# When the background work of a retention and two-FFN kernel is issued, and on which engine: a reckoned clock for each engine, GpSimd kept to the head

## The chip, the cores and the metric

The kernel runs on one core of one Trainium2 chip. The metric is the device time of one execution in microseconds (us); lower is better. The five engines run side by side: TensorE (PE) multiplies matrices, VectorE (DVE), ScalarE (ACT) and GpSimd (POOL) work on elements, and SyncE (SP) starts most DMA transfers. Each engine takes its own instructions strictly in the order in which the program issued them, so that an instruction that waits holds up everything behind it on its engine.

## The reference

```python
def _attn_ref(q, k, v):                     # 2 x 8 heads x 768 x 64
    gamma = 1.0 - 2.0 ** (-5.0 - np.arange(H, dtype=np.float32))
    for t in range(S):
        state = gamma * state + einsum('bhd,bhe->bhde', k[:, :, t], v[:, :, t])
        y[:, :, t] = scale * einsum('bhd,bhde->bhe', q[:, :, t], state)

def _moe_ref(x, w_a, w_b, w_out):           # 1536 tokens, 512 -> 1536 -> 512
    return (x @ w_a) * (x @ w_b) @ w_out

def _moe2_ref(x, w_gate, w_val, w_out, rms_g):
    xn = x / sqrt(mean(x * x, axis=-1) + 1e-06) * rms_g
    return silu(xn @ w_gate) * (xn @ w_val) @ w_out
```

Retention feeds the first feed-forward layer (FFN1, a product of two projections), whose output is normalised and goes through the second (FFN2, with a SiLU gate). The weights arrive as 64-bit integers that hold the bits of the numbers.

## The kernel before

**Precision.** A product of two float32 matrices is made of three matmuls: each operand is split into a high part, rounded to TensorE's fp32r format (`xh`, `uh`, `oh`, `hh`), and a low part, the rest (`xl`, `ul`, `ol`, `hl`). The high part is an ACT copy, the low part a subtraction on VectorE or GpSimd.

**The head** is the retention: twelve chunks of 128 tokens, with scores (`sc`, masked into `p`), a state (`st`) and results (`ya`), mixed with the first two blocks of FFN1. It ends near 77 us.

**The two FFNs** have 12 blocks `f` of 128 hidden columns each, taken in pairs. For the token blocks `j` = 0 and 1 (512 tokens each) a block is a *slot*: seven products P1, P2, P6, P7, P5, P3, P4 of sums and differences of operands, which stand for the eight of the plain method. P1, P6, P5 and P3 share one PSUM bank (A0 or A1), P2 has B0, P7 and P4 have B1. In the rows these banks are called `b`. Between P6 and P5, and between P5 and P3, ACT and VectorE must take the bank's contents (`t`) before TensorE writes on. For `j` = 2 a block is a *unit* of four plain products, a1 and a2 into one bank and b1 and b2 into a second (both `c` in the rows); the second bank of the unit is B0 before. VectorE multiplies the two into `g`. Twelve *down* products `D` of the pair before go into three banks Y0 to Y2 (`y`), which VectorE adds to the sums `acc` (ACT and VectorE copy in turn where a sum begins). Each product is six matmuls of 128x512. An even slot has the downs between its products, an odd slot has none.

**Background work** is written as generators: `conv_up` and `conv_plain` make float32 values out of the integers (`to_float`: two ACT conversions into `wt` or `u` and `v`, then three VectorE operations), form the sums of weights that the slots need (`wt`, blocks of 256 columns) and split them. `prep_t` forms and splits the differences of the tokens (`xf` or `acc` into `th`, `tl`, `xl`). `tick()`, called after every product, takes steps from the list of tasks, in order of their due times, as long as no engine's sum of estimated costs is further than LEAD beyond TensorE's. `until` forces tasks where a product needs what they make. `norm` is the normalisation between the FFNs; it runs beside the last block of FFN1, with sums of squares in `sq`.

The first set of four downs to open an FFN2 sum is a copy into an `acc` tile that held FFN1's output; `collect` therefore waits with `until` for whoever still reads that tile.

Of the kernel before, what the change touches and what calls it, by code (L numbers as in the profile page):

```python
# [16 lines left out]
P = 128  # L17
# [18 lines left out]
IDLE, LEAD = 1000, {"vec": 300, "act": 300, "gps": 3000}  # L36
# [18 lines left out]
OUTS = 3  # L55
URGENT = NF + 0.5
RS = 5
SECOND = (0, 1), (1, 1), (0, 0), (0, 2), (1, 0), (1, 2)
WAIT = 3, 2
# [4 lines left out]
def retention_glu_swiglu(ctx: ExitStack, tc: tile.TileContext, qk, kv, dq, mask, dg, eye, w1, w2, rg, out):  # L64
    nc = tc.nc

    work = dict.fromkeys(("pe", "vec", "act", "gps"), 0.0)

    class Engine:
# [15 lines left out]
    vec, act, gps = Engine(nc.vector, "vec", 150, 1.0), Engine(nc.scalar, "act", 200, 0.75), Engine(nc.gpsimd, "gps", 50, 2.3)  # L85

    def mm(out, *a, **k):
        work["pe"] += 13 + 0.4 * out.shape[-1]
        nc.tensor.matmul(out, *a, **k)  # L89
# [30 lines left out]
    for f0 in range(0, 2 * NF, G):  # L120
        ups_of = [f0 + 1] + [f0 + 2] * (f0 > 0)
        kinds += [(f, s) for f in ups_of if f < 2 * NF for s in range(2)] + [(f, 2) for f in range(f0, f0 + G)] + [(f0 + 2, s) for s in range(2) if f0 == 0]
# [16 lines left out]
    def to_float(f, s, u, follow=True):  # L139
        while (f, s) not in raws or lock:  # L140
            yield "wait"
        lock.append(f)
        raw = raws.pop((f, s)).rearrange("p (k n) t -> p k n t", k=2)
        lower, upper = raw[:, :, :, 0], raw[:, :, :, 1]
        v = cp.tile([P, DM], I32, tag="r", bufs=RS, name=f"v{f}_{s}").rearrange("p (k n) -> p k n", k=2)
        ui = u.bitcast(I32)
        act.activation(u, upper.bitcast(F32), AF.Copy, scale=2.0 ** -112)
        act.activation(v, lower.bitcast(U32), AF.Copy, scale=2.0 ** -29)
        yield
        vec.tensor_scalar(ui, ui, 3, 0x7FFFFFFF, op0=ALU.logical_shift_left, op1=ALU.bitwise_and)  # L150
        vec.scalar_tensor_tensor(ui, upper, SIGN, ui, op0=ALU.bitwise_and, op1=ALU.bitwise_or)
        if follow:
            load_w()
        yield
        add(ui, ui, v)
        lock.clear()

    def conv_plain(f, s, follow=True):
# [3 lines left out]
        u = cp.tile([P, DM], F32, tag="r", bufs=RS, name=f"u{f}_{s}").rearrange("p (k n) -> p k n", k=2)  # L162
        yield from to_float(f, s, u, follow)
        yield
# [10 lines left out]
        yield  # L175
# [6 lines left out]
    def conv_up(f):  # L182
# [4 lines left out]
        yield from to_float(f, 0, wt[:, 1:6:4, :])  # L187
        yield
        yield from to_float(f, 1, wt[:, 0:7:6, :])
        yield  # L190
        plain = f % NF < G
        if not plain:
            add(wt[:, 2], wt[:, 0], wt[:, 6])
            sub(wt[:, 3:5], wt[:, 1:3], wt[:, 0:2])
            yield
            sub(wt[:, 7], wt[:, 5], wt[:, 4])
        while may_up[0] < f:
# [3 lines left out]
        def high(a, b):  # L201
            act.copy(uh[:, a:b], wt[:, a:b])

        def low(a, b, engine=gps):
            sub(ul[:, a:b], wt[:, a:b], uh[:, a:b].bitcast(F32), engine=engine)
            w_ready.update((f, o) for o in range(a, b))

        if plain:
            for e in range(0, 2):
                both = slice(1 - e, 6 + e, 4 + 2 * e)  # L210
                act.copy(uh[:, both], wt[:, both])
                yield
                sub(ul[:, both], wt[:, both], uh[:, both].bitcast(F32))
                w_ready.update(((f, 1 - e), (f, 5 + e)))
                yield
            converting.remove(f)
            complete.add(f)
            return
        high(1, 2)
        high(4, 6)  # L220
        yield
        low(1, 2, vec)
        low(4, 6, vec)
        high(2, 4)
        yield
        low(2, 4, vec)
        high(6, 8)
        yield
        low(6, 8)
        high(0, 1)  # L230
        yield
        low(0, 1)
# [4 lines left out]
    tasks = []  # L237

    def task(due, g):
        tasks.append((due, len(tasks), g))  # L240
        tasks.sort(key=lambda t: t[:2])

    def pull(not_again=()):

        for t in list(tasks):
            if not_again.count(t) > again[0] or eager and t[0] > URGENT:
                continue
            got = next(t[2], "done")
            if got == "done":
                tasks.remove(t)  # L250
            if got != "wait":
                return t
        return None

    def until(ok):
        if ok():
            return
        while not ok():
            if not pull():
                n = [next(g, "done") for g in list(eager)]  # L260
                assert set(n) != {"wait"}
        work["pe"] = max(work.values())

    soon, again, eager = [], [0], []

    def flush():
        while soon:
            soon.pop(0)[1]()

    def tick():  # L270
# [36 lines left out]
    def prep_t(ffn, y0, y1):  # L307
# [5 lines left out]
        yield  # L313
        sub(b12, b22, b12)
        yield
        sub(b22, b22, b11)
        yield
        sub(b21, b21, b22)
        while not late:
            yield "wait"  # L320
        ts[ffn] = tuple(late["t"].tile([P, 3, 2, TB], F32R, tag=w, name=f"{w}{ffn}") for w in ("th", "tl"))
        for o, b in ((2, b22), (3, b12), (4, b11), (6, b21)):
# [4 lines left out]
            yield  # L327
            sub(lo, b, hi.bitcast(F32))
            x_ready.add((ffn, o))
            yield  # L330
# [10 lines left out]
    def rest(ffn, f, j, h, engine=gps):  # L341
# [13 lines left out]
    def unit(ffn, f, j, banks, vec_rest=False):  # L355
# [4 lines left out]
        rows = ((1, 5), (0, 6)) if ffn == 0 else ((0, 6), (1, 5))  # L360
        t = one.tile([P, TB], F32, tag=f"g{i % 2}", name=f"g{i}")
        for r, row in enumerate(rows):
            b = bank(banks[r], f"c{i}_{r}")
            for k, o in enumerate(row):
# [3 lines left out]
                if r == k == 1:  # L368
                    mult(t, t, b)
                elif k == 1:  # L370
                    act.activation(t, b, AF.Silu if ffn else AF.Copy)
                tick()
                yield
        after(1, lambda: cast(ffn, f, j, t))
        after(2, lambda: rest(ffn, f, j, t, vec if ffn == 0 and f == NF - 1 else gps))
# [80 lines left out]
    def collect(job, y, cuts):  # L456
        ffn, g, j, m = job
        if (ffn, j) not in acc:
            until(lambda: j == 0 or (0, 6) in x_ready if ffn == 0 else (1, j) in prepped and (j == 2 or (1, 6) in x_ready))
            acc[ffn, j] = held(f"acc{(2 + j) % 3}", [P, *((TPB, DM) if ffn else (KD, TB))], F32, f"acc{ffn}_{j}")  # L460
# [33 lines left out]
    def norm(j):  # L494
# [11 lines left out]
        for m in range(1, KD):  # L506
# [3 lines left out]
            add(s, s, z, engine=gps)  # L510
        for _ in range(WAIT[0]):
# [13 lines left out]
        for _ in range(WAIT[1]):  # L525
# [18 lines left out]
    with tc.manual_schedule():  # L544

        xf = {}
        with ExitStack() as att:
# [17 lines left out]
            def load_k(n):  # L565
                kv_t[n] = ap.tile([P, 2, H, D], F32, tag="kv", name=f"k{n}")
# [150 lines left out]
            def chunk(n):  # L717
# [16 lines left out]
                pull()  # L734
# [47 lines left out]
            for i, (f, j, run) in enumerate(HEAD):  # L782
# [3 lines left out]
                if j == 1 and f == 0:  # L786
                    task(G, prep_t(0, xf[0], xf[1]))
# [11 lines left out]
        late.update(dict.fromkeys(("t", "wt", "acc2", *(f"{w}{f}_2" for w in ("hh", "hl") for f in range(G))), post))  # L799
# [111 lines left out]
```

## Time and profile before

| | |
|---|---|
| median of 3 runs | 663.16 us (662.32 to 664.03) |
| the profiled execution | 663.87 us |
| its span, first to last instruction | 662.1 us |
| PE, DVE, ACT, POOL busy share of the span | 94%, 75%, 46%, 26% |
| mean granted TensorE clock | 0.992 |

The profiled execution's own time is 1.8 us above its span and 0.7 us above the median of the runs. Busy shares are means over the span; a wait of an engine is what the views of waits and of single instructions show.

### The profile page before, as it was taken

Reading aid. Unit: us, or ns where it says so; the run is one execution under the profiler, and the core shown is the slowest. Engines: PE = TensorE matmul, PEld = TensorE weight load, DVE = VectorE, ACT = ScalarE, POOL = GpSimd, SP = SyncE. Lnnn points to the kernel's source line nnn. Section 1 sums busy time; section 2 is a strip of 40 time slices with the busy share of each in tenths; the row PEclk is TensorE's granted clock in tenths of the full one; section 3 lists DMA queues with packets and bytes.
Section 4 is the critical chain, followed back from the end, with each engine's and each line's share of the span. In section 5 each row is a group of like instructions: output and inputs, shape, how many; then the busy total and the mean of one; then the engine's idle time right before and its main releaser. Section 6 shows DMA issues by size and latency. Waiting matters only on the chain. (4 is left out here: it accounts for less than half of the span.)

```text
span 662.1 us, 8640 instructions
## 1 busy us (share of the span) xinstructions
PE 625.6 (94%) x3264; PEld 509.5 (77%) x3264; DVE 497.2 (75%) x742; ACT 307.7 (46%) x573; POOL 175.1 (26%) x141
## 2 busy tenths in 40 slices
PE   8989999999989989999998989999999999999997
PEld 7778777778778778778886776877878878878886
DVE  4777696898788588599567796689889679677444
ACT  3574354644443443435345564565455265263240
POOL 2542030232340340331234221124223133132220
PEclk9999998999999999999999997999999999999999
DMA  9775012333023023124200022233312222120004
GB/s 346 308 265 188 2 62 64 96 97 96 33 63 97 32 64 96 32 64 127 64 0 1 1 63 64 65 95 96 97 34 90 66 65 74 54 63 1 0 9 182
DMA packets 16457, 54.92 MB, mean 83 GB/s; under 512 B 2080, under 2 KB 2464, under 8 KB 16416
## 3 DMA queue, kind: packets, MB, share of 16 engines
q1 hardware_dynamic: 16128, 54.21, 25.1%
q8 instruction: 25, 0.41, 0.3%
q10 hardware_dynamic: 288, 0.17, 0.1%
q14 instruction: 16, 0.13, 0.1%
HBM read 51.22 MB, written 3.15 MB: 82 GB/s over the span
## 5 line engine op out<-in xcount | busy, mean ns | idle before, releaser
L81 DVE TENSOR_TENSOR acc<-y,acc 128x512 f32<-128x512 f32 (+1 forms) x121 | 82.0, 682 | 41.2 <-PE y L89 40.5
L89 PE MATMUL c<-xh,uh 128*128 128x512 f32 x256 | 100.4, 392 | 0.2 <-ACT xh L81 0.2
L89 PE MATMUL c<-xh,ul 128*128 128x512 f32 x256 | 99.7, 389 | 0.0
L89 PE MATMUL c<-xl,uh 128*128 128x512 f32 x256 | 98.6, 389 | 0.0
L89 PE MATMUL b<-xh,uh 128*128 128x512 f32 x160 | 63.8, 399 | 13.9 <-ACT t L81 8.8
L81 DVE TENSOR_TENSOR t<-t,b 128x512 f32<-128x512 f32 x60 | 41.1, 684 | 40.1 <-ACT t L81 25.9
L81 POOL TENSOR_TENSOR hl<-t,hh 128x512 fp32r<-128x512 f32 x20 | 26.6, 1330 | 161.3 <-ACT hh L81 161.3
L81 POOL TENSOR_TENSOR ul<-wt,uh 128x512 fp32r<-128x512 f32 (+1 forms) x40 | 47.4, 1201 | 82.5 <-ACT uh L81 67.7
L89 PE MATMUL b<-xh,ul 128*128 128x512 f32 x160 | 62.4, 390 | 0.0
L89 PE MATMUL b<-xl,uh 128*128 128x512 f32 x160 | 62.3, 390 | 0.0
L81 POOL TENSOR_TENSOR hl<-g,hh 128x512 fp32r<-128x512 f32 x27 | 37.5, 1391 | 91.4 <-ACT hh L81 91.4
L89 PE MATMUL y<-hh,oh 128*128 128x512 f32 x144 | 57.1, 397 | 4.3 <-DVE acc L81 2.7
L89 PE MATMUL y<-oh,hh 128*128 128x512 f32 x144 | 57.2, 398 | 2.3 <-ACT oh L81 2.3
L89 PE MATMUL y<-ol,hh 128*128 128x512 f32 x144 | 57.5, 399 | 1.9 <-DVE ol L81 1.9
L89 PE MATMUL y<-hl,oh 128*128 128x512 f32 x144 | 56.9, 395 | 1.9 <-DVE hl L81 1.9
L89 PE MATMUL y<-oh,hl 128*128 128x512 f32 x144 | 57.0, 396 | 0.0
L89 PE MATMUL y<-hh,ol 128*128 128x512 f32 x144 | 56.7, 394 | 0.0
L89 PEld LDWEIGHTS c<-xh,uh 128*128 128x128 f32 x256 | 48.1, 188 | 10.5 <-ACT xh L81 0.4
L89 PEld LDWEIGHTS c<-xh,ul 128*128 128x128 f32 x256 | 48.0, 188 | 10.1
L89 PEld LDWEIGHTS c<-xl,uh 128*128 128x128 f32 x256 | 48.1, 188 | 9.9
L81 DVE TENSOR_TENSOR ul<-wt,uh 128x512 fp32r<-128x512 f32 (+1 forms) x62 | 53.4, 888 | 2.1 <-ACT uh L81 1.8
L81 ACT CAST uh<-wt 128x512 fp32r<-128x512 f32 (+1 forms) x102 | 50.8, 534 | 8.5 <-DVE wt L81 8.5
(97 smaller groups left out, 1262.4 us busy)
## 6 DMA issues: line engine op xcount, KB each, us to landing
raw<-in_w SPq DMA_DIRECT2D x72, 512.0 KB, 3.5
q<-in_qk SPq DMA_DIRECT2D x12, 512.0 KB, 7.2
k<-in_kv SPq DMA_DIRECT2D x12, 512.0 KB, 6.1
out<-acc SPq DMA_DIRECT2D x11, 256.0 KB, 2.0
mask_sb<-in_mask SPq DMA_DIRECT2D x1, 512.0 KB, 6.0
dq_sb<-in_dq SPq DMA_DIRECT2D x1, 256.0 KB, 8.2
out<-acc SPq DMA_DIRECT2D x1, 128.0 KB, 1.7
out<-acc ACTq DMA_DIRECT2D x1, 128.0 KB, 1.7
```

Source lines behind the costliest of these rows:

```text
L81: return getattr(self.engine, op)(out, *a, **k)
L89: nc.tensor.matmul(out, *a, **k)
```

## The change

1. **The ledger.** The sum of costs of each engine becomes a clock: an operation starts no earlier than its inputs are reckoned to be there (HOP for the way between engines), and a task carries the time at which its last step ends. A step is taken when its engine's clock and that time are below TensorE's clock plus LEAD (2300 ns for VectorE, 1750 ns for ACT). Steps are cut finer, each one tagged with its engine.
2. **GpSimd in the head alone.** All `hl` (67 operations), the last blocks of `ul` (40 operations), and the adds of squares (9) go from GpSimd to VectorE.
3. **A pair's weights in turn.** `to_float` takes both pieces of a block, ACT beginning the second before VectorE has ended the first. `conv_up` splits in six parts rather than five.
4. **Order and banks.** The unit's second bank is S, not B0, but in the last two slots of FFN1. The order of the first six units of FFN2, the homes of the FFN2 sums, the ticks waited in `norm`, the order of the weight DMAs and the due times change, and the last block's `hh` and `hl` are issued at once. The `kv` tiles get 4 buffers, and `prep_t` of FFN1 begins with chunk 8.

```diff
-IDLE, LEAD = 1000, {"vec": 300, "act": 300, "gps": 3000}
+HOP = 120
+LEAD = {"vec": 2300, "act": 1750, "gps": 4000}
...
+HOME = (2, 0, 1), (2, 1, 0)
+EARLY = {"first": 0.4, "even": 1.5, "odd": -0.5, "plain": 1.0, "out": -0.5, "second": 0.8, "t": 0.3}
+MORE = 3000
...
-SECOND = (0, 1), (1, 1), (0, 0), (0, 2), (1, 0), (1, 2)
-WAIT = 3, 2
+SECOND = ((1, 1), (0, 1), (0, 0), (0, 2), (1, 2), (1, 0))
+WAIT = {1: (4, 1), 0: (3, 2), 2: (6, 2)}
...
-                work[self.name] += self.fixed + n * self.each * (0.5 if op == "tensor_scalar" else 1)
+                at = work["pe"] + HOP if after_pe[0] is None else after_pe[0]
+                work[self.name] = max(work[self.name], at) + self.fixed + n * self.each * (0.5 if op == "tensor_scalar" else 1)
+                ends[0] = max(ends[0], work[self.name] + HOP)
...
-        yield from to_float(f, 0, wt[:, 1:6:4, :])
-        yield
-        yield from to_float(f, 1, wt[:, 0:7:6, :])
-        yield
+        yield from to_float([(f, 0, lambda: wt[:, 1:6:4, :]), (f, 1, lambda: wt[:, 0:7:6, :])])
...
+        for blocks in (slice(1, 6, 4), slice(0, 7, 6)) if plain else (slice(1, 2), slice(5, 6), slice(3, 5), slice(2, 3), slice(6, 8), slice(0, 1)):
+            act.copy(uh[:, blocks], wt[:, blocks])
+            yield "vec"
+            sub(ul[:, blocks], wt[:, blocks], uh[:, blocks].bitcast(F32))
...
+    def pull():
+        for t in list(tasks):
+            if eager and t.due > URGENT:
+                break
+            if max(work[t.on], t.ready) < work["pe"] + LEAD[t.on] + MORE * bool(eager) and t.step():
+                return True
+        return False
...
-        had = []
-        for e in work:
-            work[e] = max(work[e], work["pe"] - IDLE)
-        while all(work[e] < work["pe"] + LEAD[e] for e in LEAD):
-            t = pull(had)
-            if not t:
-                break
-            had.append(t)
+        while pull():
+            pass
...
-    def rest(ffn, f, j, h, engine=gps):
+    def rest(ffn, f, j, h, engine=vec):
...
-            until(lambda: j == 0 or (0, 6) in x_ready if ffn == 0 else (1, j) in prepped and (j == 2 or (1, 6) in x_ready))
+            until(lambda: j == 0 or (0, 6) in x_ready if ffn == 0 else (1, 2) in prepped if j == 1 else (1, 6) in x_ready)
...
-                then = unit(ffn, f, 2, (f"A{(n_slot[0] + (f % G or ffn or f < NF - G)) % 2}", "B0"))
+                then = unit(ffn, f, 2, (f"A{(n_slot[0] + (f % G or ffn or f < NF - G)) % 2}", "B0" if ffn == 0 and f >= NF - G else "S"))
```

ACT in the odd slot f = 5, before: `t` are the two contents of bank `b` that P5 and P3 wait for, `oh` and `u_2` belong to an out weight, `wt` and `v_0` to the next block's weights.

```order
L81 COPY t_1729<-b_3_1727 128x512
L81 CAST uh_1723<-wt_1564 128x256
L81 CAST oh_1777<-u_2_1741 128x512
L81 ACTIVATE wt_1780<-raw_0_1628 128x2x256
L81 ACTIVATE v_0_1781<-raw_0_1628 128x512
L81 COPY t_1729<-b_3_1727 128x512
L81 CAST hh_5_1_1814<-t_1729 128x512
```

The same place after:

```order
L87 COPY t_1739<-b_3_1737 128x512
L87 CAST uh_1731<-wt_1595 128x512
L87 CAST uh_1731<-wt_1595 128x256
L87 COPY t_1739<-b_3_1737 128x512
L87 CAST oh_1795<-u_2_1750 128x512
L87 ACTIVATE wt_1799<-raw_0_1671 128x2x256
L87 ACTIVATE v_0_1800<-raw_0_1671 128x512
```

The out weight's `oh` and the next weights' conversions stand behind the second copy of the bank now, where they stood ahead of it.

VectorE in the last block of FFN1, beside `norm` of `j` = 1, before: the adds `acc_0` and `acc_2` free the banks of the last downs, `xl_1` is the low part of FFN2's tokens.

```order
L81 TENSOR_TENSOR acc_0_983<-y_3074,acc_0_983 128x512
L81 TENSOR_TENSOR xl_1_3060<-acc_1_1123,xh_1_3059 128x1024
L81 TENSOR_TENSOR acc_0_983<-y_3092,acc_0_983 128x512
L81 TENSOR_TENSOR hl_11_2_3083<-g_2995,hh_11_2_3082 128x512
L81 TENSOR_TENSOR xl_1_3060<-acc_1_1123,xh_1_3059 128x1024
L81 TENSOR_TENSOR acc_2_1169<-y_3104,acc_2_1169 128x512
```

After:

```order
L87 TENSOR_TENSOR acc_0_985<-y_3097,acc_0_985 128x512
L87 TENSOR_TENSOR hl_11_2_3092<-g_3015,hh_11_2_3091 128x512
L87 TENSOR_TENSOR sq_3066<-sq_3066 128x512
L87 TENSOR_TENSOR xl_1_3080<-acc_1_1122,xh_1_3079 128x1024
L87 TENSOR_TENSOR ul_3110<-u_0_2797,uh_3109 128x2x256
L87 TENSOR_TENSOR ul_3110<-u_1_2822,uh_3109 128x2x256
L87 TENSOR_TENSOR acc_0_985<-y_3115,acc_0_985 128x512
L87 TENSOR_TENSOR sq_3066<-sq_3066 128x512
L87 TENSOR_TENSOR xl_1_3080<-acc_1_1122,xh_1_3079 128x1024
L87 TENSOR_TENSOR acc_2_1177<-y_3126,acc_2_1177 128x512
```

Between two adds of downs VectorE now has the add of squares and the split of FFN2's second block of weights (`ul` from `u_0`, `u_1`) as well.

VectorE at the first downs of FFN2, before: a COPY takes a bank `y` into a new sum, `wt` and `ul` belong to the weights of FFN2's third block.

```order
L81 COPY acc_1_3460<-y_3453 128x512
L81 TENSOR_SCALAR wt_3342<-wt_3342 128x2x256
L81 SCALAR_TENSOR_TENSOR wt_3342<-raw_1_2864,wt_3342 128x2x256
L81 COPY acc_1_3460<-y_3482 128x512
L81 ISA wt_3342<-wt_3342,v_1_3465 128x2x512
L81 TENSOR_TENSOR wt_3342<-wt_3342 128x256
L81 TENSOR_TENSOR wt_3342<-wt_3342 128x512
L81 COPY acc_0_3508<-y_3501 128x512
```

After:

```order
L87 COPY acc_1_3486<-y_3506 128x512
L87 TENSOR_TENSOR ul_3502<-wt_3327,uh_3501 128x256
L87 TENSOR_TENSOR ul_3502<-wt_3327,uh_3501 128x512
L87 TENSOR_TENSOR ul_3502<-wt_3327,uh_3501 128x256
L87 TENSOR_TENSOR ul_3502<-wt_3327,uh_3501 128x512
L87 TENSOR_TENSOR ul_3502<-wt_3327,uh_3501 128x256
L87 TENSOR_TENSOR tl_3445<-acc_0_985,th_3444 128x1024
L87 TENSOR_TENSOR xl_1_3080<-acc_0_985,xh_1_3079 128x1024
L87 COPY acc_2_3543<-y_3526 128x512
```

The split of the third block's weights and the last two splits of `prep_t` (`tl`, `xl`) stand between two copies of downs now.

## Rows read from the trace of the kernel before

**Rows 1.** The page's first part: busy us, share of the span, instructions of an engine.

```profile
PE 625.6 (94%) x3264; PEld 509.5 (77%) x3264; DVE 497.2 (75%) x742; ACT 307.7 (46%) x573; POOL 175.1 (26%) x141
```

**Rows 2.** TensorE's waits by releaser: us in all, times, longest.

```profile
PE b L89 <- ACT t L81: 9.6, 8, 1.5
PE b L89 <- DVE g L81: 5.1, 5, 1.7
PE ya L89 <- DVE p L81: 3.4, 8, 1.7
PE y L89 <- DVE acc L81: 2.7, 1, 2.7
PE y L89 <- ACT oh L81: 2.3, 1, 2.3
...
PE st L89 <- POOL vd L81: 1.0, 1, 1.0
```

**Rows 3.** Windows: length, busy us (instructions) of PE, PEld, DVE, ACT, POOL; clock; DMA.

```profile
90.00:110.00 20.00, 17.35 (x69) 13.84 (x69) 15.87 (x21) 9.54 (x17) 5.05 (x4) 0.91 0.18 53
...
130.00:330.00 200.00, 191.31 (x834) 155.54 (x833) 159.49 (x237) 85.97 (x158) 52.38 (x41) 1.00 0.24 72
330.00:390.00 60.00, 56.00 (x266) 45.72 (x265) 46.12 (x70) 32.86 (x48) 20.83 (x15) 1.00 0.00 1
390.00:410.00 20.00, 16.55 (x58) 12.09 (x58) 14.40 (x23) 8.09 (x14) 2.58 (x2) 0.83 0.35 105
...
430.00:460.00 30.00, 27.71 (x120) 21.78 (x119) 25.71 (x38) 18.77 (x36) 11.96 (x9) 1.00 0.30 88
460.00:662.00 202.00, 194.14 (x853) 159.45 (x851) 144.50 (x217) 84.72 (x153) 47.90 (x38) 1.00 0.20 63
```

**Rows 4.** VectorE by operation and tile: count | busy us, mean ns | idle before.

```profile
L81 DVE TENSOR_TENSOR acc<-y,acc 128x512 f32<-128x512 f32 x119 | 81.3, 686 | 40.5 <-PE y L89 39.9
...
L81 DVE TENSOR_TENSOR ul<-wt,uh 128x512 fp32r<-128x512 f32 x42 | 37.7, 901 | 0.9 <-ACT uh L81 0.9
...
L81 DVE TENSOR_TENSOR xl<-acc,xh 128x1024 fp32r<-128x1024 f32 x7 | 8.5, 1218 | 0.2 <-ACT xh L81 0.2
```

**Rows 5.** GpSimd by operation and tile, the same columns.

```profile
L81 POOL TENSOR_TENSOR hl<-g,hh 128x512 fp32r<-128x512 f32 x27 | 37.5, 1391 | 91.4 <-ACT hh L81 91.4
...
L81 POOL TENSOR_TENSOR ul<-wt,uh 128x256 fp32r<-128x256 f32 x20 | 21.2, 1062 | 4.3 <-ACT uh L81 4.3
```

**Rows 6.** The timeline in the odd slot f = 5: start, duration, instruction, [idle before].

```profile
178.99 0.62 ACT L81 CAST oh<-u 128x512 fp32r<-128x512 f32 x1 [2.27 <-DVE u L81]
...
180.62 0.58 ACT L81 COPY t<-b 128x512 f32<-128x512 f32 x1
...
181.25 0.50 PE L89 MATMUL b<-xh,uh 128*128 128x512 f32 x1 [1.44 <-ACT t L81]
181.30 0.69 DVE L81 TENSOR_TENSOR t<-t,b 128x512 f32<-128x512 f32 x1 [2.34 <-ACT t L81]
...
181.58 0.39 PE L89 MATMUL b<-xl,uh 128*128 128x512 f32 x1
...
181.81 0.40 PE L89 MATMUL b<-xh,ul 128*128 128x512 f32 x1
...
181.90 0.69 DVE L81 TENSOR_TENSOR ol<-u,oh 128x512 fp32r<-128x512 f32 x1
```

**Rows 7.** The timeline at P2 of the even slot f = 6, which follows.

```profile
190.04 2.11 DVE L81 TENSOR_TENSOR wt<-wt 128x256 f32<-128x256 f32 x2
190.21 1.40 POOL L81 TENSOR_TENSOR hl<-s,hh 128x512 fp32r<-128x512 f32 x1 [3.13 <-ACT hh L81]
...
192.81 0.50 PE L89 MATMUL b<-xh,uh 128*128 128x512 f32 x1 [1.73 <-DVE g L81]
```

**Rows 8.** The timeline at the first downs of FFN1.

```profile
94.31 4.03 DVE L81 TENSOR_TENSOR ul<-wt,uh 128x256 fp32r<-128x256 f32 x3
...
100.33 0.50 PE L89 MATMUL y<-hh,oh 128*128 128x512 f32 x1 [2.65 <-DVE acc L81]
```

More of the change, by code (lines that the diff above doesn't have):

```diff
@@ L137, in retention_glu_swiglu, with to_float @@
     lock = []
-    def to_float(f, s, u, follow=True):
-        while (f, s) not in raws or lock:
+    def to_float(pieces, follow=True):
+        while lock or pieces[0][:2] not in raws:
             yield "wait"
[L142 to L148, printed above, removed]
-        yield
[L150 to L153, printed above, removed]
-        yield
-        add(ui, ui, v)
+        lock.append(pieces)
+        n, stages = len(pieces), [None] * len(pieces)
+        for turn in range(2 * n + 3):
+            for i, (f, s, place) in enumerate(pieces):
+                k = turn - 2 * i
+                if k == 0:
+                    while (f, s) not in raws:
+                        yield "wait"
+                    raw = raws.pop((f, s)).rearrange("p (k n) t -> p k n t", k=2)
+                    u = place()
+                    v = cp.tile([P, DM], I32, tag="r", bufs=RS, name=f"v{f}_{s}").rearrange("p (k n) -> p k n", k=2)
+                    stages[i] = raw[:, :, :, 0], raw[:, :, :, 1], u, u.bitcast(I32), v
+                if 0 <= k < 4:
+                    lower, upper, u, ui, v = stages[i]
+                    if k == 0:
+                        act.activation(u, upper.bitcast(F32), AF.Copy, scale=2.0 ** -112)
+                        yield "act"
+                    elif k == 1:
+                        act.activation(v, lower.bitcast(U32), AF.Copy, scale=2.0 ** -29)
+                        yield "vec"
+                    elif k == 2:
+                        vec.tensor_scalar(ui, ui, 3, 0x7FFFFFFF, op0=ALU.logical_shift_left, op1=ALU.bitwise_and)
+                        vec.scalar_tensor_tensor(ui, upper, SIGN, ui, op0=ALU.bitwise_and, op1=ALU.bitwise_or)
+                        if follow:
+                            load_w()
+                        yield "act" if i + 1 < n else "vec"
+                    else:
+                        add(ui, ui, v)
+                        yield "act"
@@ L233, in conv_up, with __init__, step @@
         converting.remove(f)
         complete.add(f)
-    tasks = []
-    def task(due, g):
[L240 to L253, printed above, removed]
+    class Task:
+        def __init__(self, due, g):
+            self.due, self.g, self.ready, self.on = due, g, 0.0, "act"
+        def step(self):
+            was, after_pe[0], ends[0] = after_pe[0], self.ready, 0.0
+            got = next(self.g, "done")
+            after_pe[0] = was
+            self.ready = max(self.ready, ends[0])
+            if got == "done":
+                tasks.remove(self)
+            elif got in work:
+                self.on = got
+            return got != "wait"
@@ L258, in until @@
         while not ok():
-            if not pull():
+            if not any(t.step() for t in list(tasks)):
                 n = [next(g, "done") for g in list(eager)]
-                assert set(n) != {"wait"}
-        work["pe"] = max(work.values())
-    soon, again, eager = [], [0], []
+                assert set(n) - {"wait"}
+        work["pe"] = max(work["pe"], work["vec"], work["act"])
     def flush():
@@ L359, in unit @@
         n = ffn * NF + f
-        rows = ((1, 5), (0, 6)) if ffn == 0 else ((0, 6), (1, 5))
+        gate_last = n == NF and j == SECOND[0][1]
+        rows = ((1, 5), (0, 6)) if ffn == 0 or gate_last else ((0, 6), (1, 5))
         t = one.tile([P, TB], F32, tag=f"g{i % 2}", name=f"g{i}")
@@ L509, in norm @@
             act.activation(z, y[:, m], AF.Square)
-            add(s, s, z, engine=gps)
-        for _ in range(WAIT[0]):
+            add(s, s, z)
+        for _ in range(WAIT[j][0]):
             yield "tick"
@@ L524, in norm @@
         sub(rl, r, rh.bitcast(F32))
-        for _ in range(WAIT[1]):
+        for _ in range(WAIT[j][1]):
             yield "tick"
@@ L733, in chunk @@
                 step()
-                pull()
+                if n == 2 * CPT:
+                    task(G - EARLY["t"], prep_t(0, xf[0], xf[1]))
+                for t in tasks:
+                    t.step()
             start_conv(follow=False)
@@ L802, in retention_glu_swiglu @@
                 if f % NF >= G or f == NF:
-                    task(f - (0.4 if f % NF == G else 1.5 * (f % G == 0)), conv_up(f))
+                    task(f - EARLY["first" if f % NF == G else "odd" if f % G else "even"], conv_up(f))
                 else:
```

100 lines of the change are left out of this document (42 added, 58 removed).

## The prediction

> **What bounds the kernel now.** I read the page's busy shares first: TensorE is busy for 94% of the span, VectorE for 75%, GpSimd for 26% [rows 1]. So TensorE is the bound, and what can be had is its idle time and the time in which it runs at the lower clock. The view of waits then names the idle time: 9.6 us on ACT's copies `t`, 5.1 us on VectorE's products `g`, and single waits in the head and where one layer gives way to the next [rows 2]. The windows show where it lies [rows 3]. From 130 to 330 us, five pairs of FFN1, TensorE is idle for 200 − 191.3 = 8.7 us; from 460 us on, the pairs of FFN2, for 7.9 us, of which 4.4 are three waits on `t` of about 1.46 (three of the eight in rows 2) and nearly all the rest is the end, after the last matmul. Two windows show a granted clock under 1.00: 0.91 from 90 to 110 us and 0.83 from 390 to 410 us, each with a wait of over 2 us in it [rows 2, 3].
>
> A wait costs more than its idle time. A matmul lasts 0.39 us while the next begins 0.23 us after it [rows 6], and idle time is counted from the end of the last one; so each wait costs 0.39 − 0.23 = 0.16 us more.
>
> The two waits of a pair in the timeline: in the odd slot P5 waits 1.44 us for ACT's copy of its bank [rows 6]. ACT had stood in `oh`, which waited for VectorE, until 179.61 us; then came the two conversions of the next weights, and only then the copy, at 180.62 us. In the even slot P2 waits 1.73 us for bank B0, which the unit before holds until VectorE has multiplied `g`; VectorE stood in two operations on `wt` that took 2.11 us beside one of GpSimd [rows 7].
>
> **The change part by part.**
>
> *P5's wait.* ACT's copy of the bank now stands ahead of `oh` and of the conversions (the order above). It then begins when the bank is full, and TensorE has other products to do meanwhile. The three waits in FFN2 go: 4.4 + 3 × 0.16 = **4.9 us**. The same copy accounts for about half of FFN1's idle time. What is late next is `oh`; its readers are downs several products away.
>
> *P2's wait.* The unit's second bank is S, which outside `norm` nobody else uses, so P2 waits no more for `g`. With P5's waits, all eight waits of the FFN1 stretch go: 8.7 + 8 × 0.16 = **10.0 us**. Below, I take back a little for waits that stay.
>
> *VectorE takes GpSimd's work.* GpSimd took 1.06 to 1.39 us for one of these [rows 5]. 67 + 9 operations of 512 columns at 0.69 and 40 blocks of `ul`, half of 512 and half of 256 columns, at a mean of 0.56 (the 256 estimated at 0.43, from 1.22 for 1024 and 0.69 for 512 [rows 4]) are 52 + 22 = 75 us more on VectorE, 572 in all if nothing is given back. Something is: `ul` of 512 columns takes 901 ns where `acc`, which reads PSUM, takes 686 [rows 4], and three blocks of 256 took 4.03 us beside GpSimd [rows 8] where 1.3 is my estimate alone. This hides behind TensorE only if a pair's work fits. TensorE has 34 products a pair (seven and four for each of two blocks, and 12 downs) of 6 × 0.227 = 1.36 us: 46.2 us (0.227 is the pitch 0.23 to a digit more, 181.81 − 181.58 in rows 6 being rounded). VectorE has some 50 operations of 512 columns, 12 of 256 and 6 single-operand ones: for the two blocks 14 in the weights, 18 in slots and units, 6 in the out weights and 12 adds of downs. Back to back, one begins 0.60 after the other (181.30, 181.90 [rows 6]); 50 × 0.60 + 12 × 0.34 + 6 × 0.45 = 37, and 2 more for those that need the result of the one before. **39 of 46.2 us**: it fits, with 84% busy. At full durations, 0.69 apiece, it is 42.3 and still fits. So this costs nothing in the pairs, and I price it at 0, with the bound of a short queue below.
>
> Two operations of 256 columns took 2.11 us beside GpSimd [rows 7], where 2 × 0.43 is my estimate alone: work on GpSimd is not free for VectorE. The Trainium skill (Perfetto Trace Analysis, Optimizing Scalar/DVE Operations) speaks against the move in one half and for it in the other: where VectorE is saturated, some of its work may go to ScalarE or even GpSimd, it says, but the two share a port, so that this might not help. By the first half the move back would cost at least the queue's upper bound, the 6 us that I name below, and the sum would end near 645; by the second half, with which this trace agrees, it stays as it is.
>
> *The first downs of FFN1* (90 to 110 us). VectorE's 4.03 us beside GpSimd and an `xl` held up the first copy; TensorE waited 2.65 us and then ran at 0.91 on the mean of 20 us, which is 1.8 us of work [rows 2, 3, 8]. After, `prep_t` begins in the head and `xl` stands earlier, without GpSimd beside it. 2.65 + 0.16 + 1.8 = **4.6 us**.
>
> *430 to 460 us*: three waits of the same two kinds and one on `ol`, 30 − 27.7 = 2.3, with 3 × 0.16 = **2.8 us**, gone for the same reasons.
>
> *Between the layers* (330 to 410 us) is where the change also adds. Before, it loses 4.0 + 3.4 us of idle time, some 1.0 for six waits at 0.16, and 0.17 × 20 = 3.4 us of clock: 11.8 us [rows 3]; the wait for `oh` is 2.3 of it [rows 2]. That wait goes, since the out weights are converted earlier. But the work that stood there moves on. Adding up rows along the order: P5 of the last block 0.5; `rb` 0.6; the add of a down behind an `xl` (1.13) and two `ul` (0.60 each) in the norm, which hold bank Y for 2.1; another 1.0 behind the next `xl`; and at the first downs of FFN2, five `ul`, `tl` and `xl` between two copies of banks, with VectorE's 20.5 us of work against 12 downs' 16.3 of TensorE's: 4.2, and 0.7 in pieces. That is 9.1, with seven waits at 0.16 10.2. The clock may fall as it did before (3.4) or not at all; I take 1. 11.8 − 11.2 = **0.6 us**.
>
> *The head.* The waits for `p` (3.4) and `vd` (1.0) [rows 2] have to do with tiles and the place of a conversion. More `kv` buffers and `p` ahead of a conversion speak for less, a later conversion of the second weights for more. Between +1 and −3, I take **−1 us**.
>
> *What is left in the pairs.* ACT's `t` and VectorE's adds can now stand behind up to 2.3 us of background work. I take back 1 us (0 to 6).
>
> Sum: 4.9 + 10.0 + 4.6 + 2.8 + 0.6 + 1.0 − 1.0 = 22.9. The profiled execution's 663.87 becomes 641.0; it stands 0.7 above the median of the runs, so a median of **640.3 us**.
>
> **The rivals.**
> 1. *The queue between the layers clears.* My sum there adds rows in order and lets nothing overlap. If the copies of banks on ACT, half of them, let TensorE run on, about 9 of the 11.2 go: **631 us**. For it: before, VectorE was busy for just 46 of 60 us in that stretch [rows 3]. Against: the order puts seven background operations between two copies.
> 2. *The stalls there bring the lower clock, and short waits stay in the pairs.* With 0.83 over 20 us as at 390 us, twice, 6.8 rather than 1; and 0.4 in each of ten pairs: +9, **650 us**. For it: both waits above 2 us were followed by such a stretch [rows 2, 3]; against: 1.92 us of idle time within 330 to 390 us left 1.00 [rows 3].
> 3. *The waits do not go, they move.* If `t` or the copies of downs stand as late as before behind other work in one of a pair's two places, half of 14.9 stays: **648 us**; with half of 4.6 as well, 650. Against: the order puts `t` ahead.
> 4. *VectorE becomes the bound* (the other side). The place is a pair; its 39 us must pass 46.2, and to eat the gain 46.2 + 22.9/10 = 48.5. That is a mean spacing of 0.75 for each 512 columns rather than 0.60, above the durations themselves. Beyond it, each 0.05 more costs 62 × 0.05 = 3.1 us in each of ten pairs; at 0.80 **about 694 us**. For it: the 84%. Against: 0.69 is the longest that an undisturbed operation shows [rows 4, 6], and GpSimd no longer disturbs it.
>
> **How the numbers follow.** My forecast (635 to 646) 0.55; the first rival 0.18; the second 0.15, the third 0.08, the fourth 0.04. The range takes in the first two rivals: **629 to 652**, which leaves out the fourth and pieces of the others. 0.3%, 2 us, is about what a measurement of this kernel can tell from no change. Faster 0.95, same 0.02 (a third rival with the gains between the layers lost), slower 0.03.
>
> **What would show it.** Right: the waits on `t` and `g` below 3 us together; 130 to 330 us of before with TensorE's idle time under 2 us; clock 1.00 at the first downs of FFN1; VectorE at 0.69 for `ul`, near 520 us in all (572 less some 50 that no longer pass beside GpSimd, an estimate); the largest waits on `acc` between the layers, together 5 to 10 us. Wrong: waits of `y` on `acc` in every pair (VectorE's queue), idle VectorE below 5% anywhere in the pairs, or a head that has grown.

## The result and the profile after

The changed kernel takes 638.48 us (median of 4 runs, 638.38 to 638.57) against 662.99 us before (4 runs). The ratio is 0.9629, with a 95% interval of 0.9612 to 0.9646. The forecast was 640.3 us, with a range of 629 to 652. The profiled execution took 638.57 us, 25.3 us less than that of before, and its span is 25.4 us shorter.

The busy times of the engines after, from the page, stand against [rows 1]:

```profile
PE 620.4 (97%) x3264; PEld 510.5 (80%) x3264; DVE 507.3 (80%) x878; ACT 310.1 (49%) x594; POOL 26.8 (4%) x25
```

VectorE has 136 instructions more, 116 of them GpSimd's, and is busy for only 10.1 us more. TensorE's waits by releaser, against [rows 2]:

```profile
PE y L96 <- DVE acc L87: 5.0, 3, 2.1
PE ya L96 <- DVE p L87: 2.0, 7, 0.9
PE y L96 <- DVE xl L87: 1.4, 1, 1.4
PE b L96 <- ACT t L87: 1.3, 1, 1.3
```

Eight waits for `t` and five for `g`, together 14.7 us, have become one wait of 1.3. The windows after (the columns are those of [rows 3]; the two long ones are cut so that they hold as many matmuls as there):

```profile
90.00:110.00 20.00, 20.00 (x90) 16.55 (x89) 14.51 (x27) 11.02 (x23) 0.00 (x0) 1.00 0.17 53
...
130.00:320.00 190.00, 188.67 (x833) 155.89 (x832) 158.34 (x278) 86.17 (x163) 0.00 (x0) 1.00 0.24 75
...
330.00:370.00 40.00, 38.09 (x170) 31.53 (x169) 33.30 (x58) 22.32 (x33) 0.00 (x0) 0.91 0.05 14
370.00:390.00 20.00, 19.02 (x83) 15.13 (x82) 19.04 (x32) 12.13 (x23) 0.00 (x0) 1.00 0.26 79
390.00:410.00 20.00, 17.93 (x73) 14.36 (x72) 15.10 (x27) 11.13 (x21) 0.00 (x0) 0.91 0.20 58
410.00:440.00 30.00, 30.00 (x134) 24.76 (x133) 26.33 (x48) 19.19 (x37) 0.00 (x0) 1.00 0.32 103
440.00:636.70 196.70, 193.13 (x853) 159.58 (x851) 148.84 (x261) 84.46 (x158) 0.00 (x0) 1.00 0.19 62
```

The pairs of FFN1 can be read without counting waits: 833 matmuls take 190 us where 834 took 200 [rows 3]. In FFN2 853 matmuls take 196.7 us, to the end, where 853 took 202 [rows 3]. Both are stretches in which TensorE hardly waits any more: 3.57 us idle in the last window, as good as all of it after the last matmul.

VectorE's operations after, against [rows 4]:

```profile
L87 DVE TENSOR_TENSOR acc<-y,acc 128x512 f32<-128x512 f32 x119 | 81.1, 686 | 24.5 <-PE y L96 24.0
...
L87 DVE TENSOR_TENSOR ul<-wt,uh 128x256 fp32r<-128x256 f32 x80 | 32.6, 418 | 4.9 <-ACT uh L87 4.8
...
L87 DVE TENSOR_TENSOR ul<-wt,uh 128x512 fp32r<-128x512 f32 x42 | 28.8, 689 | 11.7 <-ACT uh L87 11.0
```

`ul` takes 689 ns where it took 901, while `acc`, with one input in PSUM, takes 686 as before. The Trainium skill (SBUF — State Buffer, SBUF: two separate sides) says that GpSimd and an operation of VectorE with two SBUF inputs take turns at one pair of ports, each for a whole instruction; these two rows agree.

What still waits is between the layers. The add of a down that holds bank Y at 337.5 us, in VectorE's and TensorE's timeline:

```profile
334.42 1.22 DVE L87 TENSOR_TENSOR xl<-acc,xh 128x1024 fp32r<-128x1024 f32 x1
335.56 1.29 DVE L87 TENSOR_TENSOR ul<-u,uh 128x512 fp32r<-128x512 f32 x2
336.76 0.68 DVE L87 TENSOR_TENSOR acc<-y,acc 128x512 f32<-128x512 f32 x1
```

```profile
337.50 0.50 PE L96 MATMUL y<-hh,oh 128*128 128x512 f32 x1 [1.91 <-DVE acc L87]
```

This is the `xl` and the two `ul` that the order had shown ahead of that add. The first downs of FFN2 wait 0.98 us at 385.12 and 2.07 us at 393.20, each time for a copy into `acc`.

### The profile page after: what moved, and what is told of

Its sections match the earlier page's. It is cut to its first block, busy times and chain, and to the rows that moved or that the text cites. A ratio compares the mean times of both kernels' runs of the same rounds, so it can differ in the third digit from the quotient of the medians.

```text
span 636.7 us, 8555 instructions
## 1 busy us (share of the span) xinstructions
PE 620.4 (97%) x3264; PEld 510.5 (80%) x3264; DVE 507.3 (80%) x878; ACT 310.1 (49%) x594; POOL 26.8 (4%) x25
## 4 chain that ended last, share of the span: by engine, by line
PE 85%; DVE 9%; ACT 2%; issue 2%; DMA 1%; POOL 0%; SPq 0%; DVEq 0%; ACTq 0%
PE b L96 29%; PE y L96 28%; PE c L96 24%; PE ya L96 2%; DVE acc L87 2%; DVE u L87 2%; PE sc L96 1%; DVE wt L87 1%; DMA mask_sb<-in_mask 1%; DVE p L87 1%; DVE xl L87 1%; DVE ul L87 1%; PE st L96 1%; DVE g L87 1%; PE ms L96 1%
## 5 line engine op out<-in xcount | busy, mean ns | idle before, releaser
L87 DVE TENSOR_TENSOR ul<-wt,uh 128x512 fp32r<-128x512 f32 (+1 forms) x122 | 59.4, 511 | 16.6 <-ACT uh L87 15.8
L96 PE MATMUL b<-xh,uh 128*128 128x512 f32 x160 | 62.4, 390 | 0.0
L96 PEld LDWEIGHTS c<-xh,ul 128*128 128x128 f32 x256 | 48.3, 189 | 10.7 <-DVE ul L87 0.7
L87 DVE TENSOR_TENSOR t<-t,b 128x512 f32<-128x512 f32 x60 | 41.0, 683 | 17.1 <-ACT t L87 10.7
L87 ACT CAST uh<-wt 128x512 fp32r<-128x512 f32 (+1 forms) x122 | 52.6, 479 | 2.0 <-DVE wt L87 1.8
L87 ACT ACTIVATE v<-raw 128x512 int32<-128x512 uint32 x72 | 47.9, 666 | 0.6 <-DVE u L87 0.6
L96 PE MATMUL b<-th,uh 128*128 128x512 f32 x120 | 46.9, 391 | 1.3 <-ACT t L87 1.3
L87 ACT COPY t<-b 128x512 f32<-128x512 f32 x40 | 23.5, 587 | 48.4 <-PE b L96 48.3
```

## The experiments

Ratios are to the kernel before, run on the same chip; three groups of runs had medians of before of 663.18, 663.16 and 662.35 us, the last run one of 662.88. The changed kernel was run with the first measurement of before (662.99), so differences to it, given in us, are between medians of different groups. Moving work between engines, or leaving out steps, also changes what `tick` issues next; of the runs that follow, the two that move the unit's second bank leave the order of ACT and VectorE as it was, and the others do not.

**GpSimd's work given back** to the changed kernel.

```diff
-    def rest(ffn, f, j, h, engine=vec):
+    def rest(ffn, f, j, h, engine=gps):
...
-            sub(ul[:, blocks], wt[:, blocks], uh[:, blocks].bitcast(F32))
+            sub(ul[:, blocks], wt[:, blocks], uh[:, blocks].bitcast(F32), engine=gps if not plain and blocks in (slice(6, 8), slice(0, 1)) else vec)
...
-            add(s, s, z)
+            add(s, s, z, engine=gps)
```

> The changed kernel with GpSimd's work given back: hl, the last two blocks of ul and the adds of squares are on GpSimd again, with the new ledger and banks. Theory A (the prediction: each part removes waits of its own): operations of VectorE beside GpSimd take up to 2 us again, the first downs of FFN1 wait again (up to 2.65 us, with the clock 4.6), short waits come into the pairs; 641 to 647 us. Theory B (nearly all of the gain is VectorE's freedom from GpSimd): 655 to 660 us. Theory C (the order does it all, VectorE is hidden either way): 638 to 640 us.

645.76 us (4 runs), 0.9733 (0.9713 to 0.9754): 7.3 us more than the changed kernel. Its waits:

```profile
PE y L96 <- DVE acc L87: 5.4, 2, 3.5
PE b L96 <- ACT t L87: 4.2, 2, 2.6
PE b L96 <- ACT s L87: 2.2, 2, 1.5
```

Theory A's size. But the place is not quite A's: the first downs of FFN1 do not wait (20.00 of 20 us busy from 90 to 110), and the waits for `t` and `s` come once at the first slots of each layer and at the end of FFN1 rather than pair by pair. From 130 to 320 us TensorE is busy for 188.39 of 190 us, as in the changed kernel. So the ledger and the banks clear the pairs with GpSimd at work beside VectorE.

**GpSimd's work to VectorE alone**, in the kernel before.

```diff
-    def rest(ffn, f, j, h, engine=gps):
+    def rest(ffn, f, j, h, engine=vec):
...
-        after(2, lambda: rest(ffn, f, j, t, vec if ffn == 0 and f == NF - 1 else gps))
+        after(2, lambda: rest(ffn, f, j, t, vec))
...
-        def low(a, b, engine=gps):
+        def low(a, b, engine=vec):
...
-            add(s, s, z, engine=gps)
+            add(s, s, z)
```

> The kernel before with one part of the change alone: GpSimd's work outside the head goes to VectorE, with the old ledger and banks. Theory A: P2's waits of 1.73 us shrink to the 0.37 us of the undisturbed pairs (two of them, about 3 us), the wait at the first downs of FFN1 shrinks with its clock (up to 4.6 us), P5's waits of 1.44 us stay: 655 to 659 us. Theory B: 640 to 645 us. Theory C: 661 to 664 us.

655.66 us (4 runs), 0.9874 (0.9847 to 0.9901). A's number, for another reason. The windows of this kernel:

```profile
130.00:330.00 200.00, 198.62 (x878) 163.51 (x877) 167.00 (x294) 90.65 (x165) 0.00 (x0) 1.00 0.24 72
330.00:410.00 80.00, 66.79 (x277) 53.09 (x276) 57.78 (x93) 36.18 (x54) 0.00 (x0) 0.89 0.08 27
```

In the pairs all the waits for `t` and `g` are gone, the eight in FFN1 and the three in FFN2, with the old ledger and with bank B0; one wait of 1.29 us for `oh` is new. Between the layers 13.2 us are idle where 7.45 were [rows 3], and two waits there are for FFN2's weights:

```profile
PE y L89 <- ACT oh L81: 4.6, 3, 2.8
PE c L89 <- DVE ul L81: 3.5, 1, 3.5
...
PE c L89 <- ACT uh L81: 2.5, 1, 2.5
```

This run does not separate GpSimd from the order. The old ledger now books 116 operations more on VectorE, and other background steps come at each place. ACT at the place of [rows 6], in this kernel:

```profile
175.96 0.59 ACT L81 COPY t<-b 128x512 f32<-128x512 f32 x1 [0.64 <-PE b L89]
...
180.22 0.62 ACT L81 CAST oh<-u 128x512 fp32r<-128x512 f32 x1
```

The `oh` that stood ahead of the copy stands behind it here.

**The second bank alone**, in the kernel before.

```diff
-                then = unit(ffn, f, 2, (f"A{(n_slot[0] + (f % G or ffn or f < NF - G)) % 2}", "B0"))
+                then = unit(ffn, f, 2, (f"A{(n_slot[0] + (f % G or ffn or f < NF - G)) % 2}", "B0" if ffn == 0 and f >= NF - G else "S"))
```

> The kernel before with the unit's second bank S in place of B0, nothing else. Theory A: the five waits of P2 for g go (5.1 us, with 0.16 each 5.9 us), nothing takes their place: 656 to 658 us. Theory B: g is as late as before and holds what comes next on VectorE, so at most half of it is kept: 660 to 663 us. Theory C: as A, 656 to 658 us.

658.83 us (4 runs), 0.9932 (0.9907 to 0.9956), 4.3 us less: just above A's bounds. All waits for `g` are gone, as A said, with the order of ACT and VectorE unchanged; the waits for `t` stay and are seven, 10.7 us where they were 9.6:

```profile
PE b L89 <- ACT t L81: 10.7, 7, 1.9
```

**The old bank** in the changed kernel, with the order of every engine the same.

```diff
-"B0" if ffn == 0 and f >= NF - G else "S"
+"B0"
```

> The changed kernel with the unit's second bank B0 again; the order of instructions on each engine is the same. Theory A: P2 waits for g again, but without VectorE's 2.11 us beside GpSimd only some 0.4 us, as in two pairs of before; in up to ten even slots with 0.16 each: 639 to 645 us. Theory B: g is there in time, 638 to 639 us. Theory C (the bank is what counts, whatever VectorE does): P2 waits 1.7 us in each of ten even slots, 655 us or more.

640.55 us (4 runs), 0.9657 (0.9637 to 0.9678), 2.1 us more than the changed kernel. Three waits for `g`, 2.0 us in all, the longest 0.8, and none in most pairs: A, in its lower part. The cost is rather 2.5 to 3.2 us at a like clock: two of its runs have a mean granted clock of 1.000 (640.03 and 640.14), the others 0.992 and 0.995 (641.66 and 640.96), and all runs of the changed kernel 0.991 to 0.994.

**One piece after the other** in the changed kernel.

```diff
-        for turn in range(2 * n + 3):
+        for turn in range(4 * n):
...
-                k = turn - 2 * i
+                k = turn - 4 * i
...
-                        yield "act" if i + 1 < n else "vec"
+                        yield "vec"
```

> The changed kernel with part 3 undone: to_float ends the first piece of a block before it begins the second, as before. Theory A (the prediction gave this part no term): VectorE's spare 7 us of a pair cover it; 637 to 641 us. Theory B: it is what lets ACT run ahead of VectorE, and without it ACT's copies of banks stand behind conversions again, some 0.7 us in each of ten pairs: 645 us or more.

642.07 us (4 runs), 0.9682 (0.9655 to 0.9708), 3.6 us more than the changed kernel: just over A's bounds and far from B. The pairs stay clear but for two short waits; the wait at the first downs of FFN2 is 3.21 us rather than 2.07, and the matmuls that take the changed kernel from 370.15 to 410.14 us take 2.8 us longer (371.64 to 414.41).

**The old ledger** in the changed kernel, with the costs and leads of before and one step of a task for each tick.

```diff
-LEAD = {"vec": 2300, "act": 1750, "gps": 4000}
+IDLE, LEAD = 1000, {"vec": 300, "act": 300, "gps": 3000}
...
-                work[self.name] = max(work[self.name], at) + self.fixed + n * self.each * (0.5 if op == "tensor_scalar" else 1)
+                work[self.name] += self.fixed + n * self.each * (0.5 if op == "tensor_scalar" else 1)
...
-        while pull():
-            pass
+        had = []
+        for e in work:
+            work[e] = max(work[e], work["pe"] - IDLE)
+        while all(work[e] < work["pe"] + LEAD[e] for e in LEAD):
+            t = pull(had)
+            if not t:
+                break
+            had.append(t)
```

> The changed kernel with the ledger of before (sums of costs, LEAD of 300 ns, one step of a task for each tick, the costs of before), all other parts as in the changed kernel. Theory A (of the earlier runs: in the pairs either the ledger or VectorE's freedom from GpSimd is enough; between the layers only the ledger keeps the forced steps apart): no waits in the pairs, but 8 us or more between the layers, 648 to 658 us. Theory B (the new banks, homes and order of units are what holds the waits between the layers down): 638 to 642 us.

797.26 us (6 runs), 1.203 (1.1991 to 1.2068). Neither theory had this. Its waits say why: the out weights are late everywhere.

```profile
PE y L96 <- ACT oh L87: 72.4, 18, 7.8
PE b L96 <- ACT uh L87: 21.5, 10, 5.8
```

**The same without the limit** of one step for each task and tick.

```diff
-            if t in had or eager and t.due > URGENT:
+            if eager and t.due > URGENT:
```

> The changed kernel with the ledger of before as in the run that took 797 us, but a task may take more than one step in a tick. Theory A (there the finer steps, one for each task and tick, starved the conversions, so that every out weight was late): without that limit the waits for oh go, 638 to 655 us. Theory B (sums of costs with a lead of 300 ns are what starves them): 750 us or more.

652.66 us (4 runs), 0.9853 (0.9824 to 0.9881). Theory A: it is the limit, met by finer steps, that starves the conversions. What is left of the difference, 14.2 us to the changed kernel, comes with the old ledger, its costs and its leads together: waits for `t` of 0.36 us come back in most pairs, and between the layers there are one of 5.3 for `uh` and one of 4.1 for `acc`.

**Copies of the first FFN2 downs on ACT**, and the second set of downs waiting only for the splits that read its own tile.

```diff
-            until(lambda: j == 0 or (0, 6) in x_ready if ffn == 0 else (1, 2) in prepped if j == 1 else (1, 6) in x_ready)
+            until(lambda: j == 0 or (0, 6) in x_ready if ffn == 0 else (1, 2) in prepped if j == 1 else (1, 3 if j == 2 else 6) in x_ready)
...
-            elif m % 2:
+            elif m % 2 or ffn:
```

> The changed kernel; at the first downs of FFN2 all copies of banks go to ACT (half of them were VectorE's), and the second set of downs waits only for the splits that read its own tile. Theory A (VectorE's load between two copies makes the waits at 385 and 393 us, 0.98 and 2.07 us, and their clock): most of 3.05 + 1.7 us goes, 634 to 636 us. Theory B (the load is only moved; the copies stand behind ACT's casts of th and uh, and the third set waits instead): 637 to 641 us.

639.09 us (4 runs), 0.9637 (0.9614 to 0.9661): no gain, B by its number. But the waits at 385 and 393 us are gone, and 380 to 400 us shows 20.00 us of 20 busy at clock 1.00. The third set of downs, which B named, does not wait. What took back the gain is a new wait, 40 us on:

```profile
PE y L96 <- ACT oh L87: 3.2, 1, 3.2
```

**The lead beside the normalisation** taken away.

```diff
-MORE = 3000
+MORE = 0
```

> The changed kernel with MORE = 0: beside the normalisation the background work may lead TensorE no further than elsewhere. Theory A (two ul and an xl between two adds of downs make the wait of 1.91 us at 337.5 us and the stretch of lower clock behind it): the two ul come later and 1.3 to 4.5 us go, 634 to 637 us. Theory B (what is put off is then forced at the first units of FFN2, where TensorE waits for ul): 639 to 643 us.

641.4 us (5 runs), 0.9672 (0.9649 to 0.9696), 2.9 us more than the changed kernel: B. The wait of 1.91 us shrinks to 0.74, and a first unit of FFN2 then waits 5.77 us for `ul` (the other of the two is in the head):

```profile
PE c L96 <- DVE ul L87: 6.0, 2, 5.8
```

**Copies on ACT, and the out weights of the second FFN2 pair earlier.** To the edit with the copies come:

```diff
-        kinds += [*up[0], *out_of, *up[1]] if f0 % NF == 0 else [*up[0], *up[1] * (f0 + 2 < 2 * NF), *out_of]
+        kinds += [*up[0], *out_of, *up[1]] if f0 % NF == 0 or f0 == NF + G else [*up[0], *up[1] * (f0 + 2 < 2 * NF), *out_of]
...
-                    task(g * G + G - EARLY["second" if g == NG else "out"], conv_plain(f, 2))
+                    task(g * G + G - EARLY["second" if g in (NG, NG + 1) else "out"], conv_plain(f, 2))
```

> The kernel with the copies of the first FFN2 downs on ACT, and the out weights of the second FFN2 pair fetched and converted ahead of the next weights for the slots. Theory A (the copies on ACT took away the waits at 385 and 393 us, and what they cost came back only as the wait of 3.20 us for oh at 432 us and its clock): that wait goes, 633.5 to 636 us. Theory B (ACT and VectorE have no room there, whatever goes first delays the other): uh or ul of the next block is late by as much, 638 to 641 us.

634.43 us (5 runs), 0.9582 (0.9555 to 0.9609): below the changed kernel by 4.1 us, and the intervals of the two ratios do not meet. Theory A: the wait for `oh` is gone. One of 1.00 us for `uh` is new, of the kind that B named.

**One place in ACT's order**, in the kernel before: in odd slots no background step is taken after P7.

```diff
-    def tick():
+    def tick(steps=True):
...
+        if not steps:
+            return
         had = []
...
         product(b3, "P7", True)
-        tick()
+        tick(f % G == 0)
```

> The kernel before; in odd slots no background step is taken after P7, so that ACT's copy of P5's bank stands ahead of oh and of the next conversions, and nothing else is changed. Theory A (that place in ACT's order makes the waits of 1.44 us): six waits of 1.6 us go, 653 to 656 us. Theory B (ACT is late for the same reason as VectorE, which is held up by GpSimd; the copy waits for something else, or the steps put off are late in the next slot): 659 to 664 us.

650.11 us (5 runs), 0.9812 (0.9785 to 0.9839): 12.2 us less than before, more than A expected. ACT in the odd slot of [rows 6], in this kernel:

```profile
180.11 0.59 ACT L81 COPY t<-b 128x512 f32<-128x512 f32 x1 [1.77 <-PE b L89]
180.61 0.62 ACT L81 CAST oh<-u 128x512 fp32r<-128x512 f32 x1
181.14 0.66 ACT L81 ACTIVATE wt<-raw 128x512 f32<-128x512 f32 x1
```

The copy waits for TensorE's product and nothing else. With it went the six waits of 1.4 to 1.5 us, and most waits for `g` too, though `g`'s bank and GpSimd's work are as before: FFN1's pairs have one, of 2.35 us, where four were of 0.37 to 1.74. VectorE's order is not as before, though. At P2 of the slot f = 6 the two operations on `wt` of [rows 7] stood ahead of the product `g`, which began at 192.08 us; here it is the other way round:

```profile
189.65 0.68 DVE L81 TENSOR_TENSOR g<-g,c 128x512 f32<-128x512 f32 x1
190.25 2.58 DVE L81 TENSOR_TENSOR wt<-wt 128x256 f32<-128x256 f32 x3
```

The three on `wt` still take 2.58 us beside GpSimd, but no product waits behind them.

**The same for FFN1's last block**, on top of the fastest kernel: no background step after P1 and P2 there.

```diff
-    def tick():
+    def tick(steps=True):
...
-        while pull():
+        while steps and pull():
             pass
...
         act.copy(t0, b1)
-        tick()
+        tick(n != NF - 1)
...
         add(t0, t0, b2)
-        tick()
+        tick(n != NF - 1)
```

> The kernel with the copies of the first FFN2 downs on ACT and the out weights of the second FFN2 pair earlier; besides, no background step is taken after P1 and P2 of FFN1's last block, so that ACT's copy for P5 stands ahead of an out weight's u, v and oh. Theory A (the wait of 1.34 us at 304.9 us is that place in ACT's order): 1.5 us less than the kernel without it, 632.5 to 633.5 us. Theory B (the out weight then stands ahead of the next copy, and P3 waits instead): 634 to 635 us.

634.02 us (6 runs, 633.25 to 634.88), 0.9563 (0.954 to 0.9586). By the medians this can't be told from the kernel without it (634.21 to 635.38). The wait of 1.34 us is gone, and B's appears, smaller:

```profile
306.71 0.50 PE L96 MATMUL b<-xh,uh 128*128 128x512 f32 x1 [0.37 <-ACT t L87]
```

In the profiles the clock from 320 to 360 us is 0.91 here and 1.00 without the edit, which the last section takes up. At a like clock the edit does show: runs with a mean granted clock of 0.999 or 1.000 take 633.25 to 633.70 us with it and 634.21 to 634.43 without, those at 0.994 or 0.995 take 634.34 to 634.88 with it and 635.07 and 635.38 without. That is some 0.7 us, about half of A's 1.5.

## Why the prediction was right, and where it was not

**The sum.** By the windows: FFN1's pairs 200 − 190 = 10.0 us (predicted: 10.0, less most of the 1.0 taken back). FFN2's pairs 202 − 196.7 = 5.3 (4.9). The first downs of FFN1 4.6 (4.6) and the stretch from 430 us 2.8 (2.8), by what before lost there: after, neither has idle time, and the clock is 1.00. The end of the head: the first down after it starts at 75.19 us, where it stood at 76.98, so 1.8 (1.0). Between the layers the rest of the 25.4, 0.9 (0.6). So each term was right to about 1 us. The head's is not the change's alone: the first matmul of the scores already starts at 6.83 us before and at 6.15 after, and that first down starts anywhere from 75.64 to 77.03 us in the kernel before and its three variants above, and from 75.19 to 76.09 in the changed kernel and its variants.

**The price of a wait** was set too low. The prediction took 0.39 − 0.23 = 0.16 us on top of the idle time. But the matmul behind a wait is followed after 0.33 us (181.25 and 181.58 in [rows 6]), not 0.23, which makes it 0.26: with 4.4 us of idle time, three waits are then 5.2 us, and 5.3 were measured in FFN2's pairs.

**What takes VectorE's work.** The 136 instructions more are 77 us at their durations and cost 10 us of busy time. Of the rest, 55 us came back because the operations that both kernels have are shorter (`ul` of 512 columns 901 to 689 ns, of 256 columns 862 to 418); I had put this at some 50. The other 12 are overlap: an operation of 0.69 us is followed after 0.60 [rows 6], and busy time counts the overlap once. So 507 us came out where I had named 520. That GpSimd makes the difference is borne out by the kernel with its work given back, where `ul` of 512 columns takes 958 ns. A pair fits, as the windows show; the rival with VectorE as the bound got no support.

**Which product waits** was named wrongly. The matmul of [rows 6] reads `xh`, so it is P3, which waits for ACT's copy of P5's contents; I called it P5. P5 reads `th`, and its own wait, for the copy of P6's contents, is the one that is left, at 304.3 us. The price was not touched by it, but the 0.5 us that I set for such a wait between the layers was 1.33.

**Which part removes which wait** was right for the first kind and too narrow for the second. The prediction gave P5's wait to ACT's order, and the three runs on the kernel before bear that out: where the waits of 1.4 to 1.5 us for `t` went (one place in ACT's order changed; GpSimd's work moved), `oh` had come to stand behind the copy at all six places; with bank S alone, where the order stayed, they stayed. P2's wait it gave to bank S. Bank S alone does clear it, but three of the four in FFN1's pairs also went with bank B0 and GpSimd's work as before, once VectorE's order had changed, as seen at f = 6; and in the changed kernel bank B0 brings back three waits of 2.0 us in all, where before had five of 5.1. So for P2's wait bank and order are alternatives, and its price does not belong to the bank alone. What GpSimd's work beside VectorE does to the waits of the pairs by itself is not shown. The kernel with it given back has clear pairs, so the new ledger, order and bank are enough without the move; the move alone clears them too, but it changed the order with it, and no run moves the work with the order kept.

**A pair's weights in turn** had no term. It is worth 3.6 us, 2.8 of it at the first downs of FFN2, where VectorE has next to no time to spare (19.04 of 20 us busy from 370 to 390).

**Between the layers** the sum was right (11.2 predicted, 25.4 less the other terms leaves 10.9) and its parts were not: 5.0 us of idle time where I added up 9.1, and a clock of 0.91 over 40 us and again over 20 us, 5.4 us at the face of it, where I took 1. That the errors cancel in the sum is luck. The second rival had this clock, but not clear pairs with it. The places were right: the `xl` and `ul` ahead of the add (2.1 predicted, 1.91), the two sets of first downs (1.7 and 2.5 predicted, 0.98 and 2.07). The wait for `rb` and the one behind the next `xl` (0.6 and 1.0 predicted) did not come in this execution, where the clock fell; in the kernel of the last section in which it did not, they are there with 1.19 and 0.62 us.

**The ledger** was taken as the cause of ACT's order. It is more than that: the finer steps need a tick that takes several steps of a task, for under the old limit they starve the conversions, and without that limit the old sums, costs and leads are still 14.2 us worse.

## What to carry to other kernels

Before pricing a change by the waits that its parts remove, look whether one wait can go in two ways, for then its price counts once: here P2's wait went with another bank or with another order. One well placed step can be worth much of a long list of changes: no background work just ahead of the product whose bank ACT must copy next gave 12.2 of 24.5 us. A run that takes one part alone is a test of that part only if the order of the engines' instructions is as before; where a ledger decides what is issued, read the order first. A wait that is taken away by moving work to another engine can come back where that engine's next deadline lies: the copies moved to ACT gave nothing until the out weights, needed 40 us later, were moved too, and then 4 us. And work beside GpSimd is not free: count what VectorE's operations take beside it and alone.

## What the runs showed of the hardware

The clock after the same wait differed. In the changed kernel TensorE waits 1.91 us at 337.5, and from 340 to 350 us the granted clock is 0.73, a mean over its two levels; in the kernel with the copies on ACT and the out weights earlier it waits 1.91 us at 338.1, and the clock stays at 1.00. The windows, the first of the changed kernel:

```profile
340.00:350.00 10.00, 10.00 (x40) 8.36 (x41) 7.70 (x19) 3.29 (x6) 0.00 (x0) 0.73 0.01 2
350.00:360.00 10.00, 10.00 (x54) 8.53 (x53) 7.17 (x16) 7.56 (x10) 0.00 (x0) 1.00 0.00 1
```

and the second of the other:

```profile
340.00:350.00 10.00, 9.38 (x48) 7.96 (x49) 8.16 (x19) 3.23 (x6) 0.00 (x0) 1.00 0.01 2
350.00:360.00 10.00, 8.81 (x47) 7.26 (x46) 7.64 (x16) 7.84 (x11) 0.00 (x0) 1.00 0.00 1
```

Where the clock falls, TensorE is busy throughout; where it does not, TensorE waits 0.62 us for an add and 1.19 for `rb`. The order of the matmuls is the same in both, so one and the same matmul further on can be compared, first in the changed kernel, then in the other:

```profile
360.17 0.39 PE L96 MATMUL c<-xh,uh 128*128 128x512 f32 x1
359.91 0.39 PE L96 MATMUL c<-xh,uh 128*128 128x512 f32 x1
```

It starts 22.67 us after the end of the wait where the clock fell and 21.81 where it did not. So the fall costs 0.9 us, where 0.27 of 10 us would be 2.7 in the first window alone: VectorE's and ACT's chain through the normalisation would have made TensorE wait for most of that time anyway. What a lower clock costs is only what goes beyond the waits that it replaces. What decides whether the clock falls is not settled here; the kernels differ in what stands elsewhere, and the executions of one kernel differ too (mean granted clocks of 0.994 to 1.000 in the five runs of the second).
